# Three edits to the list of tail units in a fused attention and two-FFN kernel: order within a unit, start, and own values

## The chip, the cores and the metric

The kernel runs on one core of a Trainium2 chip. The metric is device time in microseconds, the median of three runs; lower is better. TensorE (PE), VectorE (DVE), ScalarE (ACT), GpSimd (POOL) and SyncE (SP) run their own queues in order and meet on semaphores.

## The reference

Four batches, 8 heads, 576 positions, head dimension 64. Causal attention with a decay bias, then two feed-forward networks over the 2304 tokens, all in fp32.

```python
scores = scale * q @ k.T                       # 576 x 576 for each head
bias   = -(cum[:, None] - cum[None, :])        # cum = cumsum(max(s, 0))
scores = where(causal, -1e9, scores + minimum(bias, 0))
x = softmax(scores) @ v                        # -> (2304, 512)
x = (x @ w_a) * (x @ w_b) @ w_out              # 512 -> 1536 -> 512
h = x @ w_in                                   # 512 -> 2048
out = (maximum(h, 0) + alpha * minimum(h, 0)) @ w_out2
```

## The kernel before

The tokens are worked in four blocks. Blocks 0 to 2 hold the first 512 positions of batches 0 to 2; block 3 holds those of batch 3 and the last 64 positions of all four batches (256 rows), 768 in all, and is done with a seven-product scheme. Each fp32 product of the networks is three matmuls (high by high, low by high, high by low), lines 1236 to 1238 in `mm3` and 1886 to 1888 for the last network layer.

Attention is spread between the matmuls of the networks. While block b's networks run, the attention of batch b+1 for its first 512 positions is done in steps (`s01`, `s23`: scores, line 579 or 598; `av`: probabilities by values, line 842). Beside it runs a second list, the **tails**: 16 units (batch, pair of heads), each giving the last 64 positions of its batch for two heads. A unit has three steps: `ready` (loads of keys and queries, of the running sums and, for one batch, of values; the bias tile), `s4` (scores, four matmuls of 288 columns, line 777, into two PSUM banks) and `av_b` (values, 20 small matmuls, line 869, into one bank; ACT then writes `ovh` and DVE `ovl` out of the bank, lines 294 and 311). Between `s4` and `av_b` lies a chain: score reduction on DVE, exponentials on ACT, scaling, a transpose on DVE into `zt`, a DMA to DRAM (`zd`) and a DMA back into the one tile `pb`.

All order is fixed when the program is built, by a planner (`Order`) that keeps an estimated time `run.now` for TensorE and for each engine. Attention shares two PSUM banks in a ring: `slot()` takes the next one and waits, in the plan, for its last reader. `possible(f, args)` says whether a step could start at the planned time without waiting. It wants the readers of the banks done by the plan, and for `s4` and `av_b` the operands done for 3 and 7 us. `due()` is called after each group of matmuls: it takes attention steps by how far the block has come, then tail steps while the list is behind `tails_want` and the next one is possible. The list has 48 steps (16 of each kind); `tails_want` runs from 0 to 48 between the two positions in `TAILS`, counted in blocks. Where the list is behind, its next step goes out as soon as it is possible.

Buffers that matter: `pb`, `vt`, the tail's bias tile (`z4`) and its sums (`cb1`) have one copy each; `kq` has three. `v_sb` holds one batch's values; a batch's values leave it when all their uses are done (`v_uses`), and only then can those of the next batch be loaded (`load_v`). One batch of tails, `TAIL_ORDER[2]`, loads its values for each unit into `vt` (`load_vt`: a memset on POOL and six DMAs on SP, two at a time) in place of reading `v_sb`.

Of the kernel before, what the change touches and what calls it, by code (L numbers as in the profile page):

```python
# [62 lines left out]
TURN, SPACE = 1, 5  # L63


TAILS = 0.45, 2.75
TAIL_ORDER = 1, 2, 0, 3


SURE = {"s4": 3000.0, "av_b": 7000.0}  # L70


WARM = 16
# [148 lines left out]
def attention_two_moe_kernel(  # L222
# [11 lines left out]
    B, S, _ = v.shape  # L234
    H = kq_a.shape[1]
# [100 lines left out]
    def split(src, hi, lo, sbuf=True):  # L336
        yield from copy(hi, src, 0.52 if sbuf else 1.04)
        yield from sub(lo, src, f32(hi), sbuf)
# [107 lines left out]
    v_t, kq_t, cb_t, z_t, e_t = {}, {}, {}, {}, {}  # L446
    x_done = [[] for _ in range(NB)]
    reader = {}
    ring = []

    def slot():

        ring.append(ring.pop(0))
        if ring[-1] in reader:
            run.need(reader[ring[-1]])
        return ring[-1]

    def read_by(i, gen):
        reader[i] = run.spawn(gen)
        return reader[i]  # L460

    v_sb = raw.tile([P, 5, DM], F32, name="v_sb")
    nc.gpsimd.memset(v_sb[:, 4, :], 0.0)
    v_uses = {b: 2 * H // 2 if b else H // 2 for b in range(B)}

    def keys_of(b, c):
        return v[b, 0:QA, c].rearrange("(c j k) d -> j k c d", j=4, k=32)
# [37 lines left out]
    def v_used(b):  # L505
        v_uses[b] -= 1
        if not v_uses[b]:
            run.give(of_v)
# [20 lines left out]
    def load_kq(b, hp, u):  # L529

        got = []

        def chain():
            if not u and b >= STACK:
                halves = [run.spawn(stack(b, 2 * hp + j, got), run.t) for j in range(2)]
                yield halves[0]
                yield halves[1]
                return
            if b or u:
                yield of_kq  # L540
                kq = raw.tile([P, 2 * QA], F32, name="kq", tag="kq", bufs=KQ)
            else:
                kq = kq_0[hp // 2][:, hp % 2]
            got.append(kq)
            if u:
                yield from dma(kq[:, 0:S + P], kq_b[b, hp])
            else:
                r0 = 2 * hp * P + D
                yield from dma(kq, kq_a[b].rearrange("h p n -> (h p) n")[r0:r0 + P])

        kq_t[b, hp, u] = got, run.spawn(chain())

    def load_sums(b, h, u):

        got = []

        def chain():
            yield of_c1 if u else of_c0
            nk = S if u else QA
            cb = raw.tile([P, nk], F32, name=f"cb{u}", tag=f"cb{u}", bufs=1 if u else CB)  # L560
            got.append(cb)
            n = P // (u + 1)
            for j in range(u + 1):
                bh = b * H + (u + 1) * h + j
                yield from dma(
                    cb[j * n:(j + 1) * n], cum_d[bh:bh + 1, 0:nk].to_broadcast([n, nk])
                )

        cb_t[b, h, u] = got, run.spawn(chain())
# [245 lines left out]
    def settle(*keys):  # L815

        for key in keys:
            run.need(z_t[key][1])
            run.need(z_t.pop(key)[1])
            run.need(e_t.pop(key))  # L820

    def v_of(b, hp, c, j):
        o = (2 * hp + j) * D
        return v_sb[:, c, o:o + D]

    def av(b, hp):

        turned = b >= TURN
        if turned:
            settle(*((b, 2 * hp + j, r) for j in range(2) for r in (0, 2, 3)))  # L830
        else:
            run.need(*(e_t.pop((b, 2 * hp + j, c)) for j in range(2) for c in range(3)))
        while not v_t[b].done and any(args[0] == b - 1 for _, args in tails):
            tail()
        run.need(v_t[b])
        at = slot()
        pv = banks[at]
        for r in range(4 if turned else 0):
            for c in range(r + 1):
                for j in range(2):  # L840
                    p = pts[(2 * hp + j) % 4].rearrange("p (i t n) -> p i t n", i=4, n=32)
                    nc.tensor.matmul(  # L842
                        pv[64 * j:64 * j + 64, r * P:(r + 1) * P],
                        v_of(b, hp, c, j), p[:, :, r * (r + 1) // 2 + c, :],
                        start=c == 0, stop=c == r,
                    )
        for c in range(0 if turned else 4):
            for j in range(2):
                nc.tensor.matmul(
                    pv[64 * j:64 * j + 64, c * P:QA], v_of(b, hp, c, j),  # L850
                    pts[(2 * hp + j) % 4][:, AT[c]:AT[c] + QA - c * P], start=c == 0, stop=c == 3,
                )
        run.pe(4 * 1280 / 2.4)
        v_used(b)
        parts = (x[b % 2][:, hp, :] for x in (xh, xl))
        x_done[b].append(read_by(at, split(pv, *parts, False)))

    def av_b(b, hp):

        settle((b, hp, 4))  # L860
        own = v_t[b, hp] if b == TAIL_ORDER[2] else None
        run.need(own[1] if own else v_t[b])
        pb = pb_t.pop(hp)
        at = slot()
        pv = banks[at][:, 0:QB]
        for c in range(5):
            for j in range(2):
                p = pb.rearrange("p (i t n) -> p i t n", i=4, n=32)
                nc.tensor.matmul(  # L869
                    pv[64 * j:64 * j + 64],  # L870
                    own[0][0][:, c, j * D:(j + 1) * D] if own else v_of(b, hp, c, j),
                    p[:, 2 * j:2 * j + 2, c, :], start=c == 0, stop=c == 4,
                )
        run.pe(5 * 107)
        if own:
            run.give(of_vt)
        else:
            v_used(b)
        run.give(of_pb)
        parts = (x[:, hp, b * QB:(b + 1) * QB] for x in (ovh, ovl))  # L880
        x_done[NB - 1].append(read_by(at, split(pv, *parts, False)))
# [3 lines left out]
    def first_attention():  # L885
# [53 lines left out]
        for f, args in lead:  # L939
            f(*args)  # L940
        turns(1)
        av(0, 0)
        turns(2)
        av(0, 1)
        turns(3)
        av(0, 2)
        of_steps(STEPS)
        av(0, 3)
# [33 lines left out]
    def all_tails():  # L982

        def ready(b, i):
            load_kq(b, i, 1)
            load_sums(b, i, 1)
            if b == TAIL_ORDER[2]:
                load_vt(b, i)
            biases(b, i, (4,))

        units = [(b, i) for b in TAIL_ORDER for i in range(HP)]
        steps = [(ready, units[0])]
        for k, u in enumerate(units):
            steps.append((s4, u))
            if k + 1 < len(units):
                steps.append((ready, units[k + 1]))
            steps.append((av_b, u))
        return steps


    w_d = dram.tile([NW, P, WN], F32, name="w_d")
# [214 lines left out]
    units = []  # L1216
# [24 lines left out]
    o_done = {}  # L1241
    todo, want = [], 0
    tails, tails_want = all_tails(), 0.0
    tails_in = len(tails)

    def seen(*chains, margin=-100.0):
        return all(c.done and c.time + margin <= run.now for c in chains)

    def possible(f, args):
        rings = 1 if f in (av, av_b) else 2  # L1250
        if f not in (s01, s23, s4, av, av_b):
            return True
        if not seen(*(reader[i] for i in ring[:rings] if i in reader)):
            return False
        b, hp = args[:2]
        if f == av:
            keys = [(b, 2 * hp + k, r) for k in range(2) for r in (0, 2, 3)]
            return all(k in e_t and seen(e_t[k]) for k in keys) and seen(v_t[b])
        if f == av_b:
            return (b, hp, 4) in e_t and seen(  # L1260
                e_t[b, hp, 4], v_t[b, hp][1] if (b, hp) in v_t else v_t[b], margin=SURE["av_b"]
            )
        if f == s4:
            return seen(kq_t[b, hp, 1][1], z_t[b, hp, 4][1], margin=SURE["s4"])
        r = args[2] if f == s23 else 0
        return seen(kq_t[b, hp, 0][1], *(z_t[b, 2 * hp + j, r][1] for j in range(2)))
# [9 lines left out]
    def tail():  # L1276
        f, args = tails.pop(0)
        f(*args)

    def due():  # L1280

        while todo and want - (steps_in - len(todo)) > 0:
            run.pump()
            if not scarce and want - (steps_in - len(todo)) < BEHIND and not possible(*todo[0]):
                break
            step()
        run.pump()
        while tail_due():
            tail()
# [614 lines left out]
    for blk in range(NB):  # L1904
# [8 lines left out]
        steps = plan[blk][1]  # L1913
# [6 lines left out]
        for i, _ in enumerate(ffn_seven(blk, sum_x()) if blk == SEVEN else ffn(blk)):  # L1920
            want = min(steps_in, (i + 1) * steps_in * FASTER / total)
            tails_want = (blk + i / total - TAILS[0]) * tails_in / (TAILS[1] - TAILS[0])
            due()
# [65 lines left out]
```

## Time and profile before

| | us |
|---|---|
| median of three runs | 983.77 (982.96 to 983.99) |
| the profiled execution, its own time | 983.97 |
| its span, first to last instruction | 982.2 |
| PE busy in the span | 966.5 |
| DVE, ACT, POOL busy | 748.8, 560.4, 230.4 |

A busy PE is one that has a matmul in flight. Stretches where it has none are its idle time, and each has a releaser: the instruction whose end let it go on. Matmuls of 512 columns start 0.23 us apart when nothing holds them up.

### The profile page before, as it was taken

The numbers are of one execution on the slowest core, as the hardware profiler recorded it, in microseconds if no ns is written. First come the engines' busy times: TensorE is split into PE (matmuls) and PEld (weight loads), VectorE is DVE, ScalarE is ACT, GpSimd is POOL, SyncE is SP. The second block draws the span as 40 slices with busy tenths as digits, with TensorE's granted clock in tenths as the row PEclk, the third lists the DMA queues.
The fourth block names the chain that finished last, engine by engine and source line by source line (L and its number), as shares of the span: only waits on it lengthen the run. The fifth ranks groups of instructions, "written<-read, shape, count | busy, mean of one in ns | idle before, by whom it ended". The sixth has DMA issues, their size and how long they took to land.

```text
span 982.2 us, 15766 instructions
## 1 busy us (share of the span) xinstructions
PE 966.5 (98%) x5267; PEld 811.9 (83%) x5267; DVE 748.8 (76%) x1719; ACT 560.4 (57%) x1168; POOL 230.4 (23%) x280
## 2 busy tenths in 40 slices
PE   7999999999999989999999999999999999999997
PEld 6677877777888878888888888888899999999896
DVE  8897969878677787987577666976597888787782
ACT  7866767657655555756455464754452333576453
POOL 3141113222345243562034353540000000000000
PEclk9999999999999999999999999999999999999999
DMA  7489997988698969678588766555312213011202
GB/s 264 136 295 315 382 354 267 308 286 305 230 317 267 300 209 310 200 253 282 175 279 253 212 210 209 183 156 161 118 32 98 65 65 103 28 65 65 65 1 64
DMA packets 125442, 193.61 MB, mean 197 GB/s; under 512 B 33968, under 2 KB 62896, under 8 KB 125360
## 3 DMA queue, kind: packets, MB, share of 16 engines
q1 hardware_dynamic: 115568, 174.78, 54.8%
q10 hardware_dynamic: 9792, 17.83, 4.8%
q8 instruction: 41, 0.67, 0.3%
q14 instruction: 41, 0.34, 0.1%
HBM read 148.98 MB, written 43.59 MB: 196 GB/s over the span
## 4 chain that ended last, share of the span: by engine, by line
PE 92%; DVE 3%; DMA 2%; ACT 1%; issue 1%; ACTq 0%; POOL 0%; SPq 0%; POOLq 0%; DVEq 0%
PE bank L1236 21%; PE bank L1237 20%; PE bank L1238 20%; PE bank L1886 4%; PE bank L1888 4%; PE bank L1887 4%; PE bank L842 3%; PE bank L1739 2%; PE bank L1738 2%; PE bank L1740 2%; PE bank L579 2%; PE bank L777 1%; DVE z L302 1%; PE bank L598 1%; PE bank L869 1%; PE bank L804 1%
## 5 line engine op out<-in xcount | busy, mean ns | idle before, releaser
L1236 PE MATMUL bank<-xh,wh 128*128 128x512 f32 (+1 forms) x620 | 239.5, 386 | 1.3 <-DVE sm L302 1.3
L1237 PE MATMUL bank<-xl,wh 128*128 128x512 f32 (+1 forms) x620 | 234.3, 378 | 0.0
L1238 PE MATMUL bank<-xh,wl 128*128 128x512 f32 (+1 forms) x620 | 234.2, 378 | 0.0
L294 ACT ACTIVATE wh<-raw 128x512 fp32r<-128x512 f32 (+1 forms) x199 | 116.1, 594 | 143.8 <-PE bank L1237 62.3
L1236 PEld LDWEIGHTS bank<-xh,wh 128*128 128x128 f32 x620 | 116.3, 188 | 25.5 <-issue 3.3
L1238 PEld LDWEIGHTS bank<-xh,wl 128*128 128x128 f32 x620 | 116.3, 188 | 19.5
L1237 PEld LDWEIGHTS bank<-xl,wh 128*128 128x128 f32 x620 | 116.4, 188 | 18.3
L311 DVE TENSOR_TENSOR wl<-raw,wh 128x512 fp32r<-128x512 f32 (+1 forms) x141 | 89.4, 647 | 46.0 <-ACT wh L294 44.9
L311 POOL TENSOR_TENSOR wl<-raw,wh 128x512 fp32r<-128x512 f32 x63 | 87.1, 1385 | 79.6 <-ACT wh L294 62.9
L286 ACT ACTIVATE z<-z,mn 128x128 f32<-128x128 f32 (+4 forms) x144 | 82.7, 576 | 19.0 <-DVE mn L302 18.8
L1236 PE MATMUL bank<-gh,wh 128*128 128x512 f32 (+1 forms) x240 | 90.5, 377 | 0.0
L1237 PE MATMUL bank<-gl,wh 128*128 128x512 f32 (+1 forms) x240 | 88.9, 371 | 0.0
L1238 PE MATMUL bank<-gh,wl 128*128 128x512 f32 (+1 forms) x240 | 88.7, 370 | 0.0
L1017 ACT ACTIVATE top<-raw 128x512 f16<-128x512 bf16 x90 | 69.0, 784 | 14.5 <-DMA raw<-in_w_dram 13.3
L1886 PE MATMUL bank<-wh,gh 128*128 128x512 f32 x192 | 76.2, 397 | 0.0
L1887 PE MATMUL bank<-wl,gh 128*128 128x512 f32 x192 | 74.8, 390 | 0.0
L1888 PE MATMUL bank<-wh,gl 128*128 128x512 f32 x192 | 74.8, 390 | 0.0
L294 ACT ACTIVATE gh<-g 128x512 fp32r<-128x512 f32 x84 | 52.5, 625 | 31.2 <-DVE g L302 30.4
L311 DVE TENSOR_TENSOR gl<-g,gh 128x512 fp32r<-128x512 f32 x68 | 55.1, 810 | 11.4 <-ACT gh L294 10.5
L311 POOL TENSOR_TENSOR wl<-w,wh 128x512 fp32r<-128x512 f32 x26 | 34.3, 1319 | 109.1 <-ACT wh L294 83.8
L321 DVE TENSOR_SCALAR z<-z,sm 128x512 f32<-128x512 f32 (+4 forms) x100 | 56.8, 594 | 1.1
L302 DVE STREAM_TRANSPOSE zt<-z 128x384 f32<-128x384 f32 (+2 forms) x88 | 55.5, 646 | 1.9 <-DMA zd<-zt 1.1
(155 smaller groups left out, 1916.7 us busy)
## 6 DMA issues: line engine op xcount, KB each, us to landing
raw<-w_d SPq DMA_DIRECT2D x91, 512.0 KB, 4.4
raw<-in_w_dram SPq DMA_DIRECT2D x90, 512.0 KB, 5.9
kq<-in_kq_a_dram SPq DMA_DIRECT2D x24, 512.0 KB, 6.5
w_d<-w ACTq DMA_DIRECT2D x46, 256.0 KB, 5.7
zd<-zt SPq DMA_DIRECT2D x48, 192.0 KB, 4.1
pt<-zd SPq DMA_DIRECT2D x48, 192.0 KB, 4.4
zd<-zt SPq DMA_DIRECT2D x24, 256.0 KB, 3.5
pt<-zd SPq DMA_DIRECT2D x24, 256.0 KB, 4.8
```

The lines of the kernel that those rows point to most:

```text
L286: nc.scalar.activation(o, i, func, **k)
L294: nc.scalar.activation(o, i, AF.Copy, scale=by)
L302: f(*args, **k)
L311: (nc.gpsimd if eng == "pool" else nc.vector).tensor_tensor(o, i0, i1, op=ALU.subtract)
L321: (nc.gpsimd if eng == "pool" else nc.vector).tensor_scalar(o, i, s0, s1, op0=ALU.mult, op1=ALU.mult)
L1017: nc.scalar.activation(top.bitcast(F16).rearrange("p (n t) -> p n t", t=2)[:, :, 1], r.bitcast(BF16)[:, 4:4 + 4 * WN].rearrange("p (n t) - ...
L1236: nc.tensor.matmul(o, wh, ih, start=first, stop=False)
L1237: nc.tensor.matmul(o, wh, il, start=False, stop=False)
L1238: nc.tensor.matmul(o, wl, ih, start=False, stop=last)
L1886: nc.tensor.matmul(acc[t], gh[:, c], wh, start=first, stop=False)
L1887: nc.tensor.matmul(acc[t], gh[:, c], wl, start=False, stop=False)
L1888: nc.tensor.matmul(acc[t], gl[:, c], wh, start=False, stop=last)
```

## The change

Three things. A tail unit's `s4` and the next unit's `ready` now come ahead of the preceding unit's `av_b`, so that the list reads s4(1), ready(2), av_b(0), s4(2), ready(3), av_b(1), and so on. The list begins at 0.75 of block 0 in place of 0.45 and still ends at 2.75; the batches come in the order 0, 2, 1, 3 in place of 1, 2, 0, 3. Batches 0 and 1 load their own values into `vt` (batch 0 alone before), so the values of batch 1 leave `v_sb` when its `av` steps are done. Beside this, `possible` wants the reader of a bank done 2 us before a tail's `s4` or `av_b` (0.1 us after, before).

```diff
-TAILS = 0.45, 2.75
-TAIL_ORDER = 1, 2, 0, 3
-SURE = {"s4": 3000.0, "av_b": 7000.0}
+TAILS = 0.75, 2.75
+TAIL_ORDER, OWN = (0, 2, 1, 3), (0, 1)
+SURE = {"bank": 2000.0, "s4": 3000.0, "av_b": 7000.0}
...
-    v_uses = {b: 2 * H // 2 if b else H // 2 for b in range(B)}
+    v_uses = {b: H // 2 if b in OWN else H for b in range(B)}
...
-        while not v_t[b].done and any(args[0] == b - 1 for _, args in tails):
+        while not v_t[b].done and b - 1 not in OWN and any(x[0] == b - 1 for _, x in tails):
             tail()
...
-        own = v_t[b, hp] if b == TAIL_ORDER[2] else None
+        own = v_t[b, hp] if b in OWN else None
...
-            if b == TAIL_ORDER[2]:
+            if b in OWN:
                 load_vt(b, i)
...
             steps.append((s4, u))
             if k + 1 < len(units):
                 steps.append((ready, units[k + 1]))
-            steps.append((av_b, u))
-        return steps
+            if k:
+                steps.append((av_b, units[k - 1]))
+        return steps + [(av_b, units[-1])]
...
-        if not seen(*(reader[i] for i in ring[:rings] if i in reader)):
+        spare = SURE["bank"] if f in (s4, av_b) else -100.0
+        if not seen(*(reader[i] for i in ring[:rings] if i in reader), margin=spare):
             return False
```

## Rows read from the trace of the kernel before

**Rows 1.** The page: engines' busy time; shares of the chain that ended last.
```profile
PE 966.5 (98%) x5267; PEld 811.9 (83%) x5267; DVE 748.8 (76%) x1719; ACT 560.4 (57%) x1168; POOL 230.4 (23%) x280
PE 92%; DVE 3%; DMA 2%; ACT 1%; issue 1%; ACTq 0%; POOL 0%; SPq 0%; POOLq 0%; DVEq 0%
```

**Rows 2.** Stretches: us, PE, PEld, DVE, ACT, POOL busy (instructions), clock, DMA share, GB/s.
```profile
350.00:375.00 25.00, 23.73 (x103) 19.72 (x104) 20.66 (x58) 11.30 (x27) 8.62 (x11) 0.93 0.77 251
142.00:260.00 118.00, 115.67 (x618) 91.31 (x617) 92.93 (x197) 80.93 (x151) 32.29 (x36) 1.00 0.84 286
260.00:472.00 212.00, 209.44 (x1116) 171.22 (x1116) 170.36 (x391) 123.19 (x256) 86.68 (x103) 0.99 0.82 265
472.00:692.00 220.00, 220.00 (x1234) 180.87 (x1230) 152.84 (x361) 116.46 (x247) 78.30 (x96) 1.00 0.65 201
```

**Rows 3.** Waits of PE from 142 to 692: total us, times, longest.
```profile
PE bank L777 <- DVE ovl L311: 3.6, 2, 2.6
PE bank L1236 <- DVE sm L302: 1.3, 1, 1.3
```

**Rows 4.** Timeline of PE, three stalls: start, length, instruction, [idle before, releaser].
```profile
170.09 0.50 PE L1236 MATMUL bank<-xh,wh 128*128 128x512 f32 x1 [1.32 <-DVE sm L302]
...
227.74 0.75 PE L777 MATMUL bank<-kq 128*128 128x288 f32 x2 [1.01 <-DVE ovl L311]
...
348.06 0.65 PE L777 MATMUL bank<-kq 128*128 128x288 f32 x2
351.27 1.33 PE L777 MATMUL bank<-kq 128*128 128x288 f32 x2 [2.56 <-DVE ovl L311]
354.40 0.40 PE L1238 MATMUL bank<-gh,wl 128*128 128x512 f32 x1
```

**Rows 5.** Timeline of PE: an `s4` that waits for nothing, and what follows.
```profile
162.83 1.13 PE L777 MATMUL bank<-kq 128*128 128x288 f32 x4
164.95 0.39 PE L1238 MATMUL bank<-xh,wl 128*128 128x512 f32 x1
```

**Rows 6.** Timelines of DVE and POOL around the stall at 348.
```profile
345.18 2.39 DVE L311 TENSOR_TENSOR kl<-kq,kh 128x512 fp32r<-128x512 f32 x2
351.00 0.21 DVE L311 TENSOR_TENSOR ovl<-bank,ovh 128x64 fp32r<-128x64 f32 x1
...
345.67 4.73 POOL L311 TENSOR_TENSOR wl<-raw,wh 128x512 fp32r<-128x512 f32 x3 [0.70 <-ACT wh L294]
```

**Rows 7.** Timeline of DVE around the stall at 168.
```profile
163.77 0.45 DVE L302 CUSTOM_DVE_ANT_0 z<-bank,z 128x288 f32<-128x288 f32 x1
169.39 0.65 DVE L302 SCALAR_TENSOR_TENSOR g<-bank,m 128x512 f32<-128x512 f32 x1
```

**Rows 8.** Tails: instructions of `s4` and `av_b`: duration ns min/median/max, first to last start.
```profile
L777 PE MATMUL bank<-kq x64: 403/405/847, 162.8 to 644.0; 128*128 128x288 f32 x64
L869 PE MATMUL bank<-pb,v_sb x240: 222/222/270, 191.8 to 673.6; 128*64 128x64 f32 x120
```

**Rows 9.** Own values: the DMAs of `vt`, POOL's wait ahead of its memset.
```profile
vt<-in_v_dram SPq DMA_DIRECT2D x16, 64.0 KB, 3.9
457.62 1.35 SPq L327 DMA_DIRECT2D vt<-in_v_dram  x2
464.32 1.13 SPq L327 DMA_DIRECT2D vt<-in_v_dram  x2
457.66 0.20 POOL L496 MEMSET vt<- 128x128 f32 x1 [2.46 <-PE bank L869]
```

**Rows 10.** Waits of SP's queue over the whole run: total us, times, longest.
```profile
SPq L327 <- DVE wl L311: 208.6, 36, 21.8
SPq L327 <- PE bank L869: 13.5, 4, 7.4
```

**Rows 11.** An `av` and the last DMA that it needs.
```profile
324.60 1.31 SPq L327 DMA_DIRECT2D pt<-zd  x2
332.75 0.44 PE L842 MATMUL bank<-pt,v_sb 128*64 128x128 f32 x4
```

## The prediction

> **What bounds the kernel.** I read the engines' busy times first. PE has a matmul in flight for 966.5 of 982.2 us, and 92% of the chain that ended last is PE's own work [rows 1]. The matmuls are the same after the change, so only PE's idle time, and time at a lower clock, can be won: 15.7 us at most. Then I looked where that idle time lies. The steps that the change touches begin at about 139 us; from 142 to 692 PE is idle for 2.3 us in the first stretch, 2.6 us in the second, nothing in the third [rows 2]. The rest is the start of the kernel and its end, which the change doesn't reach. The waits of PE in this stretch have two causes: twice a tail's `s4` waits for `ovl`, 3.6 us together, and once a network matmul waits for DVE, 1.3 us [rows 3]. No PE wait on a DMA, on weights or on values is among them, though DVE is busy for about 80% of blocks 0 and 1 and the DMA engines for over 80% [rows 2].
>
> The timeline gives the size of each [rows 4]. At 168 PE idles 1.32 us, at 227 1.01 us, at 348 2.56 us. The third costs more than its idle time: the granted clock of 350 to 375 is 0.93 where its neighbours have 1.00 [rows 2], that is a part of the stretch at 1.2 in place of 2.4 GHz, after the idle time. From the first score matmul to the sixth network matmul behind it are 354.40 - 348.06 = 6.34 us; the same eleven starts in an `s4` that waits for nothing take 164.95 - 162.83 = 2.12 us [rows 4, 5]. So this one stall costs 4.22 us. Together: 1.32 + 1.01 + 4.22 = 6.55 us, **0.67% of the run, and all that the change can plainly win**.
>
> **Edit 1, scores ahead of the preceding unit's values, with 2 us of margin on a bank.** Both long waits have one form. `av_b` of one unit takes one of the two banks, and `s4` of the next takes both. In the old list they are neighbours, and the list is late: the first and last `s4` lie 162.8 and 643.4 us into the run, 480.6 us for 15 units, 32.0 us each [rows 8] (644.0 is the last of its four matmuls, some 0.6 us behind the first), where `TAILS` asks for 3 x 2.3/48 = 0.144 blocks, 31 us for blocks of some 217 us. A late list puts out its next step as soon as the plan calls it possible, so `s4` follows `av_b` at once. The plan is optimistic about DVE: before 351.00, when `ovl` ran, DVE did two subtractions of 1.2 us each [rows 6], for which the plan holds 155 + 1.04 x 512 ns = 0.69 us, and other work. In the new list there lie a `ready` and an `av_b` between two `s4`, and 2 steps of 2/48 x 217 = 9 us each between an `av_b` and the next `s4`, if the list is on time. It can be: from `s4` to `av_b` took 191.8 - 162.8 = 29 us for the first unit and 673 - 643 = 30 us for the last [rows 8], and the new order leaves five steps, 45 us. The list's pace becomes 3 x 2.0/48 x 217 = 27 us, no longer bound by a chain that must end before the next begins. Both waits on `ovl` then go: -1.01 and -4.22 us. The margin alone would not do it: `ovl` was 2.56 us late for the second, 2 us cover only most of that.
>
> The Trainium skill, "SBUF — State Buffer", section "Who interferes with whom", has VectorE operations with two inputs in SBUF and GpSimd operations exclude each other on a shared port. The two `kl` subtractions beside POOL's three `wl` agree [rows 6]: by that rule the lateness of a bank's reader comes with POOL's work, wherever a tail step is put, and 2 us are no bound for it. That speaks for the rival "the list stays late" below.
>
> **Edit 2, start at 0.75 of block 0.** The list's first steps move from 139 to about 205 us. The stall at 168 is a network matmul that waits behind DVE's queue: `g` is written at 169.39, and in that queue stand the first unit's two score reductions of 0.45 us [rows 7], their two small read-outs and the join, some 1.2 us, just before. Without them `g` is about 1.2 us earlier, and 1.32 us of idle time shrink to 0.1; I book -1.3, bound 0 (other DVE work moves up) to -1.3. What this work meets later: 16 units now lie in 2.0 blocks in place of 2.3, so 8 units to a block in place of 7. A unit's DVE work is an estimated 4 to 5 us (two reductions of 0.45 [rows 7]; a scaling, a transpose and `ovl` at no more than the 1.2 us of a subtraction [rows 6]), hence DVE of block 1 goes from 170 to about 175 of 212 us [rows 2]. Block 2 ran at 153 of 220 with no idle PE, block 1 at 170 with one stall, and that of the `s4` kind, so I cost the density at 0, with 0 to 4.2 us as bounds: one long wait as the one at 348.
>
> **Edit 3, own values for batches 0 and 1.** It adds 4 units x 6 = 24 DMAs and four memsets of 0.20 us [rows 9]. The DMAs go on SP, some 0.6 us each, 15 us of a queue that waits for other engines most of the time: 208.6 us for DVE's `wl` alone [rows 10]. What stands behind them on SP are weights (fetched ahead; PE has no wait for them) and the transposed probabilities. The memset waits on POOL for the preceding `av_b`, 2.46 us at 457 [rows 9], and `wl` stands behind it; PE didn't wait there. One copy of `vt` makes a chain: three rounds of DMAs begin at 457.6 and 464.3 for the first and third, and with 3.9 us to land the last is there some 12 us after `av_b` [rows 9]; with the 7 us of `SURE`, 19 us, under the pace of 27. Cost on PE: 0. In return batch 1 leaves `v_sb` when its `av` steps end, and the loads of batch 2 come earlier; no PE wait on `v_sb` stands in the trace, so the gain is 0 too.
>
> **A new wait.** With scores ahead, a unit's `zd` is ready before the preceding `av_b`, and its load into `pb` is now issued right at the planned `av_b`. Where PE is later than the plan, SP stands at that DMA until PE has read `pb`: 15 times. The nearest row is SP waiting for L869 at `vt`: 13.5 us in 4 times, 7.4 at most [rows 10]. What then comes late are the loads of `pt`; the tightest `av` of block 1 began at 332.75, and its last `pt` was issued at about 325.9 (the second of two from 324.60) [rows 11]; with no less to land than the 3.9 us of the smaller `vt` [rows 9] it has at most 2.9 us of slack. A mean wait of 3.4 us uses up the slack of the tightest `av`, not of one issued some us earlier: mostly hidden. I take 0, bounds 0 and the 4.2 us of a long wait for each `av` hit.
>
> **The sum.** 1.32 + 1.01 + 4.22 = 6.55 off. But every queue from 139 to 700 us is put in another order, and the plan stays as optimistic as it was: I leave two short waits of the old size, 1.32 + 1.01 = 2.3 us, in the new order. Net -4.2 us. The profiled execution (983.97, 1.8 us over its span) and the median (983.77) agree within 0.2, so from the median: 983.8 - 6.55 + 2.3 = **979.5 us**.
>
> **Rivals.**
> - *All gone* (part of the forecast's range): no wait is left, 983.8 - 6.55 = 977.2; with half the spread of the runs (982.96 to 983.99) under it, 976.7.
> - *The list stays late.* Own values, the margins and one `pb` hold the steps back, `s4` again follows an `av_b` closely, and the change doesn't do what it says. The margin still takes 2 us: 2.56 becomes 0.56 without the fall of the clock, 1.01 goes. Then 977.2 + 0.6 + 2.3 = 980.1, faster all the same. For it: the port. Against: five steps of room for a chain of 29 us.
> - *The wait moves.* `av_b` is now followed by an attention step, whose margin is still -0.1 us, and a late `ovl` holds that in place of `s4`. One long wait and the two short ones: 977.2 + 4.2 + 2.3 = 983.7, **no change**. For it: `ovl` was 2.6 us late once, 1.0 another time [rows 3, 4]. Against: in the old trace no attention step waited for a tail's bank in this stretch [rows 3].
> - *SP stops at `pb`.* Three or more of the 15 new waits outlast the slack of `av`, each with a fall of the clock: 977.2 + 3 x 4.2 = 989.8, with two and one short wait 986.9, **slower**. It decides from two on. For it: a wait of 7.4 us was seen. Against: mean 3.4, and most `av` have more slack.
>
> **Chances.** Forecast with "all gone" 0.52, the late list 0.12, the moved wait 0.23, SP 0.13. The measurement tells about 0.2% (2 us) from no change: faster under 981.8, slower over 985.7. The first two are faster, the third no change but for its edges (0.02 to slower), the fourth slower: 0.64, 0.21, 0.15. The range 976.7 to 986.0 leaves out SP's case and a little at the lower end.
>
> **What would show it.** Right: no PE wait of L777 on `ovl`; the first L777 near 215 us in place of 163 and the last L869 near 650; units 27 us apart; no idle PE at 168; granted clock 1.00 throughout blocks 0 to 2; 48 DMAs and 8 memsets of `vt`; SP waits for L869 in number, with no L842 behind a `pt`. Wrong: an idle PE of over 2 us ahead of L579, L842 or L869, a stretch of clock under 0.95, or a network matmul waiting for `g` or `wl` in the denser blocks.

## The result: 0.76% slower

| | us, median | ratio to the kernel before | 95% interval |
|---|---|---|---|
| before | 983.77 (980.07 to 984.36, 5 runs) | | |
| after | 990.85 (988.85 to 991.56, 5 runs) | 1.0076 | 1.0061 to 1.0090 |

The prediction was 979.5 in a range of 976.7 to 986.0. The span of the profiled execution went from 982.2 to 989.7 us, by 7.5 us. PE's matmuls are the same, so the loss is idle time or clock. The page of the kernel after and its stretches (us; PE, PEld, DVE, ACT, POOL busy, with instructions; granted clock; DMA share; GB/s) show where:

```profile
PE 969.3 (98%) x5267; PEld 813.5 (82%) x5267; DVE 750.9 (76%) x1720; ACT 558.2 (56%) x1165; POOL 224.5 (23%) x286
...
142.00:260.00 118.00, 116.48 (x590) 92.64 (x589) 95.97 (x189) 79.38 (x147) 24.06 (x29) 1.00 0.86 286
260.00:480.00 220.00, 212.19 (x1155) 172.48 (x1155) 166.80 (x396) 125.44 (x261) 88.98 (x111) 0.98 0.80 257
480.00:720.00 240.00, 240.00 (x1325) 197.71 (x1322) 166.50 (x382) 124.19 (x261) 78.31 (x101) 1.00 0.63 199
...
310.00:330.00 20.00, 16.00 (x80) 12.62 (x80) 12.24 (x43) 8.75 (x23) 4.18 (x8) 0.91 0.92 301
350.00:370.00 20.00, 16.42 (x68) 12.71 (x67) 17.78 (x48) 9.87 (x24) 9.52 (x12) 0.91 0.78 273
```

The loss is in block 1. From 260 to 480 PE is idle for 7.8 us, where it was idle for 2.6 in the same block before [rows 2]: 5.2 us more. The granted clock of that block is 0.98 against 0.99, another 2 us. Two stretches of 20 us hold 7.6 of the 7.8 us, both with a clock of 0.91, that is with a part at 1.2 GHz. Block 0 has 0.8 us less idle time than before, block 2 none, as before. PE's waits from 142 to 720, total, times, longest (before: [rows 3]):

```profile
PE bank L579 <- DVE ovl L311: 4.0, 1, 4.0
PE bank L579 <- DVE mn L302: 2.4, 2, 1.9
PE bank L1237 <- DVE g L302: 1.4, 1, 1.4
PE bank L777 <- DVE ovl L311: 1.2, 1, 1.2
```

The first and longest wait is an attention step (line 579) that needs the bank of an `av_b`; in the old trace it was the tail's own `s4` (line 777). So the reader of that bank, `ovh` on ACT and then `ovl` on DVE, is late again. The timelines of PE, ACT and DVE around the two stretches tell why:

```profile
318.21 0.33 PE L579 MATMUL bank<-kl,qs 128*128 128x384 f32 x1
322.54 0.44 PE L579 MATMUL bank<-kh,qs 128*128 128x384 f32 x1 [4.00 <-DVE ovl L311]
324.12 0.63 PE L1238 MATMUL bank<-xl,wh 128*128 128x512 f32 x1
...
357.13 0.75 PE L777 MATMUL bank<-kq 128*128 128x288 f32 x2 [1.17 <-DVE ovl L311]
362.61 0.30 PE L579 MATMUL bank<-kh,qs 128*128 128x128 f32 x1 [1.93 <-DVE mn L302]
...
312.71 0.62 ACT L294 ACTIVATE wh<-raw 128x512 fp32r<-128x512 f32 x1
320.73 0.77 ACT L646 ACTIVATE z<-cb,cumq 128x576 f32<-128x576 f32 x1 [7.39 <-DMA cb<-cum_d]
321.41 0.76 ACT L1018 ACTIVATE top<-raw 128x512 f16<-128x512 bf16 x1
322.04 0.19 ACT L294 ACTIVATE ovh<-bank 128x64 fp32r<-128x64 f32 x1
...
350.92 0.52 DVE L642 TENSOR_SCALAR z<-cb,cumq 128x576 f32<-128x576 f32 x1 [6.33 <-DMA cb<-cum_d]
356.86 0.22 DVE L311 TENSOR_TENSOR ovl<-bank,ovh 128x64 fp32r<-128x64 f32 x1
```

ACT stands idle for 7.39 us with the bias of a coming tail unit at the head of its queue (`z<-cb`, 576 columns), because that unit's running sums have not landed. `ovh`, which empties the bank, stands two places behind it. Thirty us later DVE stands the same way for 6.33 us with `ovl` behind it. PE meets the full bank at 318, idles for 4.00 us, and comes back at the lower clock (matmuls 0.63 us long at 324 against 0.39). The second stretch has two steps. At 355 a tail's `s4` waits 1.17 us for `ovl`, with the clock still at 1.00; the score reduction of that `s4` then comes late out of the same DVE queue, which shows no idle time from 350.92 to 363, and the next attention step waits 1.93 and 0.47 us for it. The clock falls behind that, 0.83 from 360 to 370.

The same lines stand in the trace of before, and I had not looked for them. This is ACT ahead of the stall at 227 and DVE ahead of the stall at 348:

```profile
220.45 0.78 ACT L646 ACTIVATE z<-cb,cumq 128x576 f32<-128x576 f32 x1 [4.21 <-DMA cb<-cum_d]
226.70 0.19 ACT L294 ACTIVATE ovh<-bank 128x64 fp32r<-128x64 f32 x1
...
340.26 0.52 DVE L642 TENSOR_SCALAR z<-cb,cumq 128x576 f32<-128x576 f32 x1 [3.74 <-DMA cb<-cum_d]
```

### The profile page after: what moved, and what is told of

It is laid out like the page before. It is cut to its first block, busy times and chain, and to the rows that moved or that the text cites. A ratio compares the mean times of both kernels' runs of the same rounds, so it can differ in the third digit from the quotient of the medians.

```text
span 989.7 us, 15807 instructions
## 1 busy us (share of the span) xinstructions
PE 969.3 (98%) x5267; PEld 813.5 (82%) x5267; DVE 750.9 (76%) x1720; ACT 558.2 (56%) x1165; POOL 224.5 (23%) x286
## 4 chain that ended last, share of the span: by engine, by line
PE 91%; DVE 3%; DMA 2%; ACT 1%; SPq 1%; issue 1%; POOL 0%; ACTq 0%; POOLq 0%; DVEq 0%
PE bank L1237 20%; PE bank L1238 20%; PE bank L1239 20%; PE bank L1888 5%; PE bank L1890 4%; PE bank L1889 4%; PE bank L842 3%; PE bank L1741 2%; PE bank L1740 2%; PE bank L1742 2%; PE bank L579 2%; DMA cb<-cum_d 1%; PE bank L777 1%; PE bank L598 1%; PE bank L869 1%; DVE z L302 1%
## 5 line engine op out<-in xcount | busy, mean ns | idle before, releaser
L311 DVE TENSOR_TENSOR wl<-raw,wh 128x512 fp32r<-128x512 f32 (+1 forms) x146 | 93.7, 655 | 49.5 <-ACT wh L294 48.9
L311 POOL TENSOR_TENSOR wl<-raw,wh 128x512 fp32r<-128x512 f32 x58 | 78.5, 1356 | 66.8 <-ACT wh L294 61.1
L311 DVE TENSOR_TENSOR gl<-g,gh 128x512 fp32r<-128x512 f32 x65 | 52.8, 812 | 10.8 <-ACT gh L294 10.2
L294 ACT ACTIVATE wh<-w 128x512 fp32r<-128x512 f32 x66 | 41.0, 627 | 27.0 <-DVE w L302 12.5
L302 DVE SCALAR_TENSOR_TENSOR w<-raw,top 128x512 int32<-128x512 int32 x68 | 48.6, 726 | 6.4 <-ACT top L1018 5.0
```

The lines of the kernel that those rows point to most:

```text
L294: nc.scalar.activation(o, i, AF.Copy, scale=by)
L302: f(*args, **k)
L311: (nc.gpsimd if eng == "pool" else nc.vector).tensor_tensor(o, i0, i1, op=ALU.subtract)
```

## The experiments

Theory A: the new order within a unit puts a bias operation just ahead of the preceding unit's output, so that a late load of sums holds a bank. Rival B: the 24 more loads of own values make the sums late. Rival C: the denser list loads the engines too much. Names with a- start from the changed kernel, with b- from the kernel before. The ratios are to runs of the kernel before from the same session; these spread from 977.9 to 987.5 us over all sessions, so a single trace shows one course of several, and differences of a few us rest on the intervals.

| run | us, median | ratio to before | 95% interval |
|---|---|---|---|
| after, old order within a unit | 1008.3 | 1.0252 | 1.0231 to 1.0273 |
| before, new order alone | 979.1 | 0.9958 | 0.9942 to 0.9975 |
| after, own values for batch 0 alone | 980.1 | 0.9971 | 0.9953 to 0.9989 |
| after, bias behind the values | 982.8 | 1.0000 | 0.9986 to 1.0015 |
| after, batches 1, 2, 0, 3 | 990.1 | 1.0078 | 1.0049 to 1.0107 |
| after, one load of own values | 980.0 | 0.9973 | 0.9953 to 0.9993 |
| after, sums planned 6 us later | 979.6 | 0.9964 | 0.9947 to 0.9980 |
| before, sums planned 6 us later | 981.0 | 0.9983 | 0.9967 to 0.9998 |
| before, margin of 2 us alone (not the reference's output) | 983.6 | 1.0007 | 0.9990 to 1.0023 |
| after, own values issued from ACT | 984.2 | 1.0014 | 1.0000 to 1.0027 |
| before, new order and sums later | 978.4 | 0.9956 | 0.9939 to 0.9973 |
| after, one batch's own values and sums later | 989.1 | 1.0069 | 1.0049 to 1.0090 |
| after, same bytes in two loads | 979.0 | 0.9962 | 0.9946 to 0.9978 |
| after, start 0.45, batches 1, 2, 0, 3 | 977.9 | 0.9944 | 0.9929 to 0.9959 |

**The changed kernel with the old order.**

```diff
-            if k:
-                steps.append((av_b, units[k - 1]))
-        return steps + [(av_b, units[-1])]
+            steps.append((av_b, u))
+        return steps
```

> The changed kernel with the old order within a unit put back (values of a unit ahead of the scores of the next); start, own values and margin stay as changed. Theory A (the new order puts the bias operation of the unit after next, which waits for its running sums, just ahead of the values' output of this unit in the queues of ACT and DVE, so that a late load of sums holds a bank and with it PE): the two long stalls near 318 and 355 to 367 go, 981 to 986 us. Rival B (the 24 more loads of own values, in the stretch where the DMA engines are busiest, make the sums late): 988 to 991 us, with long waits of a bias operation for the sums still there. Rival C (the denser list loads DVE too much): 988 to 991 as well, with waits on DVE's own work.

1008.3 us: no theory had that. Its waits of PE are at the end of block 2:

```profile
PE bank L869 <- DMA pb<-zd: 23.9, 3, 9.1
...
717.49 1.34 PE L869 MATMUL bank<-pb,v_sb 128*64 128x64 f32 x20 [9.04 <-DMA pb<-zd]
```

With the old order a unit's chain of some 29 us must end before the next one's scores, and 27 us to a unit are not to be had. The list falls behind, and its last units are done in a row at the end of block 2, each with PE waiting for `pb`. So the new order is what makes the later start possible at all. It says nothing for A: the long waits in block 1 are gone, but so is the place of everything else.

**The kernel before with the new order alone.** The edit is the one above, the other way round, on the kernel before.

> The kernel before with the new order within a unit alone; start at 0.45, batches 1, 2, 0, 3, one batch with own values, no margin. A: slower than before, 986 to 991 us, with waits of PE on a bank whose reader stands behind a bias operation. B and C: 980 to 984 us.

979.1 us, 0.42% faster, where A expected slower; B and C had 980 to 984. The span of the profiled execution is 976.6 us, 5.6 less than before (the medians differ by 2.9); no `s4` or attention step waits for a bank, the bias of a tail waits for nothing, and PE's waits from 142 to 720 are these:

```profile
PE bank L1237 <- DVE sm L302: 2.0, 2, 1.3
```

So the order, without the margin, takes the waits on `ovl` away as predicted. Theory A in its first form, that the order by itself brings the bias ahead of the output, falls.

**The changed kernel with own values for batch 0 alone.**

```diff
-TAIL_ORDER, OWN = (0, 2, 1, 3), (0, 1)
+TAIL_ORDER, OWN = (1, 2, 0, 3), (0,)
```

> The changed kernel with own values for batch 0 alone and the batches in the old order 1, 2, 0, 3; order within a unit, start and margin stay as changed. B: 981 to 985 us, and the waits of a bias operation for the sums shrink below 3 us each. A: 987 to 991 us. C: 988 to 991 us.

980.1 us, on B's side and 0.9 under its range: some 10 us come back, the waits of a bias for the sums are 1.3 to 1.9 us, and one wait of PE for `ovl`, 1.0 us, is left. It changes the order of the batches with it, since batch 1 can't come third with its values in `v_sb`; the next but one parts the two.

**The changed kernel with the bias behind the values.** The bias of the next unit becomes a step of its own after `av_b`.

```diff
-            biases(b, i, (4,))
...
-        steps = [(ready, units[0])]
+        steps = [(ready, units[0]), (biases, (*units[0], (4,)))]
...
             if k:
                 steps.append((av_b, units[k - 1]))
+            if k + 1 < len(units):
+                steps.append((biases, (*units[k + 1], (4,))))
```

> The changed kernel with the bias of the next unit made in a step of its own, behind the values of the unit before; its loads stay where they are. A: the bias operation no longer stands ahead of the values' output, so no long wait of PE on a bank in 200 to 700: 979 to 985 us. B: the sums still come late and hold other work of the same queues: 987 to 991 us.

982.8 us, 8 less than the changed kernel, all loads in place. No PE wait over 1.4 us is left from 142 to 720, and a bias waits 1.5 us at most. B's loads alone would have left the time where it was. So both seem needed: loads that make the sums late, and a bias that stands ahead of the output.

**The changed kernel with the old order of the batches.**

```diff
-TAIL_ORDER, OWN = (0, 2, 1, 3), (0, 1)
+TAIL_ORDER, OWN = (1, 2, 0, 3), (0, 1)
```

> The changed kernel with the batches in the old order 1, 2, 0, 3, own values still for both 0 and 1. It parts edit 3 in two: batch order alone, or loads of own values. If the own loads themselves, in the stretch from 205 to 340 where the DMA engines are busy for over 80%, make the sums late: 987 to 992 us, as the changed kernel, since batch 1 now loads its own there. If it is the order of the batches: 979 to 983 us.

990.1 us with the same two stalls (PE waits 3.0 and 2.3 us for `ovl`). It isn't the order of the batches; the first batch of tails to be done, whichever it is, loads its own values in the stretch where this hurts.

**The changed kernel with one load of own values in each unit.**

```diff
-            yield {"pool": 240}, SEEN
-            nc.gpsimd.memset(vt[:, 4, :], 0.0)
-            for i in range(0, 4, 2):
-                yield from dmas(*((vt[j::4, 0:4, :], keys[j]) for j in range(i, i + 2)))
...
+            yield {"pool": 820}, SEEN
+            nc.gpsimd.memset(vt, 0.0)
+            yield from dma(vt[0::4, 0:4, :], keys[0])
```

> The changed kernel with one of the six loads of own values in each unit, the rest of that tile zeroed by one memset (five sixths of the loads of own values are left out, so the values of batches 0 and 1 in the tails are not complete). If it is the number of DMAs on SP and on the DMA engines: 978 to 983 us, no bias operation waits over 3 us for its sums. If only the place of the tails counts: 987 to 992 us.

980.0 us; no bias waits for its sums, and PE has one wait from 142 to 720:

```profile
PE bank L1233 <- DVE g L302: 1.4, 1, 1.4
```

The list, the start and the margins are those of the changed kernel, so the loads of own values are a cause. Every edit makes the planner lay all queues anew, so one fast variant could be luck. That all of them are is unlikely: one batch less, one load, fewer loads, a later bias and the old start all bring the time to 978 to 983, and the other order of the batches, laid anew too, keeps both stalls.

**The plan's estimate for the sums, in both kernels.** One number: the plan takes the sums of a tail to land 6 us later. No work is added; the bias is queued later.

```diff
                     cb[j * n:(j + 1) * n], cum_d[bh:bh + 1, 0:nk].to_broadcast([n, nk])
                 )
+            if u:
+                yield {"cum": 0.0}, 6000
```

> The changed kernel with one number of the plan changed: it holds the sums of a tail to land 6 us later than it did, so that the bias operation is put later in the queues of ACT and DVE; all DMAs stay. If PE's long waits come from a bias operation that stands ahead of the values' output and waits for sums: those waits go, 979 to 984 us. If PE waits because DVE, ACT or SP have too much to do: 987 to 992 us.

> The kernel before with that one number changed. Its stalls at 227 and 348 (1.0 and 4.2 us) had a bias operation that waited 4.2 and 3.7 us for sums ahead of the late output. If that is their cause they go: 977 to 981 us. If they come from the neighbourhood of scores and values alone, as the prediction held: 982 to 985 us.

979.6 us for the changed kernel, 11 less with nothing else touched: DVE, ACT and SP can do their work, so C falls; what costs is who stands at the head of a queue. 981.0 for the kernel before, 0.17% less, at the upper end of what was expected: the stalls at 227 and 348 are gone, and a wait of 2.4 us of an `s4` for an `av`'s output has come in their place. So the old stalls too had the bias as their likely cause, though here the interval nearly reaches 1.

**Own values issued from ACT.** The same loads, planned and issued on ACT.

```diff
-                yield from dmas(*((vt[j::4, 0:4, :], keys[j]) for j in range(i, i + 2)))
+                yield from act_dmas(*((vt[j::4, 0:4, :], keys[j]) for j in range(i, i + 2)))
...
+        yield {"act": 330}, 700
+        nc.scalar.dma_start(o, i)
```

> The changed kernel with the loads of own values issued from ACT's queue in place of SP's; the same 48 loads and bytes. If they cost by standing in SP's queue ahead of the sums: 979 to 984 us and no wait of a bias operation over 3 us. If they cost on the DMA engines, whoever issues them: 987 to 992 us, with such waits still there. ACT gets 48 issues of some 0.4 us, 19 us of a queue that is idle for 43%, and may now stand at a load that waits for the tile: up to 986 by that.

984.2 us, between the two expectations: a bias still waits 1.0 to 3.4 us for sums, but PE waits for no `ovl`. The longest of its waits are for `g`, 1.8 us at 274 and the 1.4 us at 169 that the other runs with the later start have too. So this alone didn't decide.

**The same bytes in two loads.**

```diff
-            for i in range(0, 4, 2):
-                yield from dmas(*((vt[j::4, 0:4, :], keys[j]) for j in range(i, i + 2)))
-            yield from dmas(
-                *((vt[j::4, 4, :], v[b, QA + 32 * j:QA + 32 * j + 32, own]) for j in range(2))
-            )
+            yield from dmas(
+                (vt[:, 0:4, :], v[b, 0:QA, own].rearrange("(c p) d -> p c d", p=P)),
+                (vt[0:QB, 4, :], v[b, QA:S, own]),
+            )
```

> The changed kernel with the six loads of own values of a unit put together as two that move the same bytes (the rows then lie in another order than the probabilities want, so the values of batches 0 and 1 in the tails are mixed up). If the number of DMAs that stand in SP's queue is what delays the sums: 978 to 983 us, as with one load. If the bytes on the DMA engines do it: 987 to 992 us.

979.0 us, with 16 loads for 48 and all the bytes. So it is not their bytes. The edit also issues a unit's loads in one round in place of three, so the number of loads and their rounds are not parted. In this run block 1 has no idle PE, with the DMA engines busier than in the kernel after. The block, and the second halves of the sums of the two units that were late, in this run and under the last "..." the second of them in the kernel after (the first, 311.88, stands further below):

```profile
260.00:480.00 220.00, 220.00 (x1226) 180.41 (x1225) 175.57 (x405) 131.42 (x272) 91.06 (x115) 1.00 0.86 269
...
305.79 1.06 SPq L327 DMA_DIRECT2D cb<-cum_d  x1
334.77 0.91 SPq L327 DMA_DIRECT2D cb<-cum_d  x1
...
345.17 0.47 SPq L327 DMA_DIRECT2D cb<-cum_d  x1
```

From issue to landing these took 7.2 and 8.1 us here, 8.8 and 5.7 in the kernel after. So the transfers are about as long; SP issues them 6 and 10 us later in the kernel after, and that makes the sums late. With the loads issued from ACT the same two go out at 308.84 and 338.80, in between.

**The old start with own values for both batches.**

```diff
-TAILS = 0.75, 2.75
-TAIL_ORDER, OWN = (0, 2, 1, 3), (0, 1)
+TAILS = 0.45, 2.75
+TAIL_ORDER, OWN = (1, 2, 0, 3), (0, 1)
```

> The changed kernel with the start put back to 0.45 and the batches in the order 1, 2, 0, 3; own values still for 0 and 1. If own values cost wherever their loads lie: 985 to 992 us. If only the meeting of the later start with own values costs (own loads at the change of block, 205 to 340 us): 978 to 983 us.

977.9 us, 0.56% faster than before and the lowest median of all runs, with all 48 loads. Against the run at 990.1 only the start differs. The loads of `vt` and the first `av_b` that reads it in this kernel, and under the "..." the loads in the changed kernel (ns min/median/max, first and last start):

```profile
L869 PE MATMUL bank<-pb,vt x160: 222/222/270, 199.5 to 544.9; 128*64 128x64 f32 x160
L327 SPq DMA_DIRECT2D vt<-in_v_dram x48: 484/614/1112, 139.2 to 521.0; - x48
...
L327 SPq DMA_DIRECT2D vt<-in_v_dram x48: 489/613/877, 213.4 to 555.3; - x48
```

A unit's loads begin when the `av_b` before it has read `vt`: here at 139, 200 and every 30 us after, so that the fourth unit's begin at about 260; in the changed kernel the first begin at 213 and the fourth unit's lie between 324 and 342, ahead of the second stall. So own values cost where they meet the later start, not by themselves.

**The kernel before with the margin of 2 us on a bank alone.** The margin that comes with the first edit, without the new order. It was expected at 980 to 984 us if, as the prediction held, the margin doesn't do what the order does, and at 977 to 980 us if it were the active part.

983.6 us, no change. This kernel doesn't give the reference's output, for a reason that stays open, so its time counts for little; its waits are still of use. Both waits on `ovl` are gone and block 1 has no idle PE, but the list ends later, and its last unit waits for `pb` at the end of block 2:

```profile
706.24 1.33 PE L869 MATMUL bank<-pb,v_sb 128*64 128x64 f32 x20 [5.23 <-DMA pb<-zd]
```

**Two that were meant as better versions.** The first is the kernel before with the new order and the later estimate for the sums; the second is the changed kernel with own values for batch 0 alone and that estimate.

> The kernel before with the new order within a unit and the sums planned to land 6 us later. A candidate: with both causes of the old stalls treated, 977 to 980 us; if the order alone had already taken all that was to be had, the same as the order alone, 978 to 981 us.

978.4 us: within its expectation, no better in its interval than the order alone.

> The changed kernel with own values for batch 0 alone, the batches in the order 1, 2, 0, 3, and the sums planned to land 6 us later. A candidate: 977 to 981 us. If the later start itself costs something (all waits on sums gone by either cure), it stays a few us above the order alone.

989.1 us, a miss, and by another wait than any so far. The timeline of PE:

```profile
346.15 0.80 PE L871 MATMUL bank<-pb,v_sb 128*64 128x64 f32 x20
354.85 2.40 PE L844 MATMUL bank<-pt,v_sb 128*64 128x128 f32 x20 [7.90 <-DMA v_sb<-in_v_dram]
```

(lines 871 and 844 are `av_b` and `av` here). With the later start, batch 1's tails hold `v_sb` into block 1; 6 us more in the plan push them past the point where batch 2's first `av` wants its own values. This is what own values for batch 1 are good for, and the trace of before didn't show it.

## Why the prediction was wrong, point by point

**What bounds the kernel** held. PE's idle time in blocks 0 to 2 was all that could be won, 6.55 us with the clock that it costs, and the loss lies there too.

**Edit 1** held in size, not in cause, which is luck. I booked 5.2 us for the two waits on `ovl`, and the order alone took both away, 5.6 us off the span of one execution, 0.25 to 0.58% in the medians (2.5 to 5.7 us). It did so in a trace where no tail's bias waits for sums at all; no run parts that from the wider spacing of steps that I argued with. That the margin alone would not take both waits away is not borne out: its run has neither. And I put the lateness of `ovl` down to a plan that is optimistic about DVE's own work, from two long subtractions [rows 6]. The idle time of DVE and ACT just ahead of it, 3.74 and 4.21 us behind a load of sums, was in the same timelines. Reading a busy queue's work and not the last idle time in it was the first failed step; with it I would have asked of each edit what it does to that load.

**Edit 2**: the 1.3 us at 168 didn't go, PE still waits 1.4 us for `g` there with no tail near, while the run with the old start, new order and all own values has no wait there. In the kernel after, DVE's scaling of `m` takes 1.52 us beside POOL's `wl`, and 0.47 three us later:

```profile
166.99 1.52 DVE L321 TENSOR_SCALAR m<-m,alpha_sb 128x512 f32<-128x512 f32 x1
170.09 0.47 DVE L321 TENSOR_SCALAR m<-m,alpha_sb 128x512 f32<-128x512 f32 x1
...
165.53 2.69 POOL L311 TENSOR_TENSOR wl<-w,wh 128x512 fp32r<-128x512 f32 x2 [0.17 <-PE bank L1239]
```

I had given the bound (0) and taken the other end. The Trainium skill, "SBUF — State Buffer", section "Who interferes with whom", lets one of VectorE and GpSimd block the other for a whole instruction where they want the shared port; this row agrees, with 1 us.

**Edit 3** is the step that failed: cost on PE 0, from the argument that SP waits for other engines most of the time [rows 10] and that what stands behind the loads are weights and probabilities. The sums of the next unit and batch stand behind them too, and they were left out of the list. What a queue's mean idle time can't show is who waits for the one transfer behind. The timeline of SP in the kernel after, and from its chain the load that ACT waited for:

```profile
305.47 1.13 SPq L327 DMA_DIRECT2D vt<-in_v_dram  x2
306.69 0.54 SPq L327 DMA_DIRECT2D kq<-in_kq_b_dram  x1
307.28 0.48 SPq L327 DMA_DIRECT2D cb<-cum_d  x1
311.88 1.46 SPq L327 DMA_DIRECT2D cb<-cum_d  x1
...
311.88 8.76 DMA cb<-cum_d
```

The last two loads of own values stand right ahead of the unit's keys and sums, and the second half of the sums, issued at 311.88, took 8.76 us. Measured cost: 990.9 against 977.9 to 980.1 with fewer loads, one batch less or the old start, 11 to 13 us. The path, as far as the traces show it, is the issue on SP: against the run with two loads the sums are issued 6 and 10 us later, and their transfers are not much longer. The loads' own issue (1.1 us for a pair at 305.47) explains a part of it. The rest is how SP's queue is laid out and where it stands: 4.9 us at a `zd` that waits for DVE just ahead of 305 (5.0 us in the run with two loads too), and 4.0 us within the last pair of loads ahead of the second unit's sums, 336.79 to 341.76, until a transfer of `w_d` had landed. How much each adds is not shown.

**The new wait at `pb`** cost nothing, as booked: SP waits for L869 16.3 us in 7 times in place of 13.5 in 4.

**The rivals.** "The wait moves" had the right place, an attention step behind an `av_b` whose reader is late, but one such wait at 4.2 us; there were two stretches of it, 4.0 and 3.6 us of idle time and, at a clock of 0.91 over 20 us, some 1.8 us more in each, and the time left the range. "SP stops at `pb`" gave the right sign for a reason that didn't occur. "The list stays late" occurred where the new order was taken away, and I had priced a late list only by its bank waits, not by its last units in a row at the block's end: 1008 us. The margin of 2 us by itself takes the bank waits away and puts a wait for `pb` of 5.2 us at the end of block 2 in their place, in the one run that tried it, which doesn't give the reference's output.

## What to carry to other kernels

Where a reader of a buffer is late, look for the last idle time in its engine's queue ahead of it, not at the work that happened to run: in an in-order queue an operation that waits for a DMA delays all that stands behind it, here a 0.2 us copy that held PE for 4 us and cost it part of its clock. For each DMA that is added, list the transfers behind it in its queue with the operations that wait for them. And try the edits of one change apart: here one was worth 0.4%, and another, whose loads stood ahead of the sums in SP's queue, took more than that back.

## What the runs showed of the hardware

Six loads of 64 and 16 KB, issued in three rounds, in place of two of the same bytes in one round cost 11 us in the kernel after. The DMA engines were busy for 0.80 of block 1 with the six and 0.86 with the two, and the second halves of the two units' sums behind them landed 8.8 and 5.7 us after their issue with the six, 7.2 and 8.1 with the two: what moved was the issue.

A fall of the clock to a mean of 0.91 over 20 us came behind an idle time of 4.00 us, and behind 1.17, 1.93 and 0.47 us within 8 us; none came behind the waits of 1.4 us. The length of one wait doesn't settle it: a PE wait of 2.4 us, with 0.4 us more right behind it, is followed by such a fall in the changed kernel with the later sums (0.91 from 380 to 400), one of 2.4 us by none in the kernel before with the later sums (1.00 from 330 to 350).
